# Corner placement of the state-times-q products, and a new order of loads and early weight conversions, in a retention layer followed by two MLPs

## Chip, cores and metric

The kernel runs on one core of a Trainium2 chip. The metric is the device time of one launch in microseconds. The engines are named as in the profile: PE (TensorE matmul), PEld (its weight loads), DVE (VectorE), ACT (ScalarE), POOL (GpSimd) and SP (the queue that issues most transfers).

## The reference, cut to what matters

Retention over 2 batches, 8 heads, 768 positions and head size 64, in blocks along the sequence, with a state carried from block to block; its output, 1536 tokens by 512 channels, goes through two MLPs of 512 to 2048 to 512.

```python
for b in range(nb):
    intra = einsum('bhic,bhjc->bhij', qb, kb) * Dmask
    intra = einsum('bhij,bhjd->bhid', intra, vb)
    inter = einsum('bhid,bhde->bhie', qb * lam_pow, kv_state)
    out[:, :, sl] = intra + inter
    kv_state = lam_block * kv_state + einsum('bhsd,bhse->bhde', kb * rev_pow, vb)
h = x @ w_in;  g = max(h, 0) + alpha * min(h, 0);  x = g @ w_out
h = x @ w_in2; g = max(h, 0) ** 2;                 out = g @ w_out2
```

## The kernel before, in words

**Retention.** The kernel takes chunks of 128 positions, so there are 6 chunks and 2 batches, 12 steps n (`ORDER`, L40), with the batches alternating. A step has four groups of eight float32 products, one per head; the heads go in four pairs `a`, and `t` is the head's place in its pair. `scores(n)` (L393 to L406) multiplies k by q into the tile `s`; `decay(n)` (L408) multiplies that by the decay mask on DVE. `outputs(n)` (L427) holds the other three: `o` from v and the masked scores (L436), `o` from the state and q (L444, from n = 2 on), which adds to the same PSUM tile, and `pk` from r and v (L459, `products`), which is the state's increment; r is k with its rows reversed. `factors(n)` scales q and r on POOL (L418, L421), two steps ahead. In L444 head t takes partitions 64t to 64t+63 of the contraction and writes the same partitions of the output, so it uses two corners of the array: top left and bottom right.

**Leaving PSUM.** `keep_output` writes `o` rounded to fp32r (`xah`, ACT, L469); `keep_rest` writes the remainder (`xal`, L479): on DVE, or, in a step that also converts weights, on POOL from a full copy that ACT made (`whole`, L472). `keep_state` adds `pk` to the decayed old state (DVE, L485) and decays the new state for two steps later (`old`, four ACT instructions, L491).

**Weights.** The weights come as float64 bits, in 64 pieces of 512 KB (`load_piece`, `raw`). A conversion makes a high and a low fp32r part, in program order: L127 and L128 on ACT (`start`), L134 and L135 on DVE (`begin`), L143 on DVE and L145 on ACT, which writes `wh` (`middle`), L154 on DVE, which writes `wl` (`end`). `SEQ` is the order of the pieces. Four conversions lie inside retention, at the steps that `EARLY_UNITS` (L44) marks; `EARLY_LOADS` (L45) marks the steps at which a piece is loaded on SP. The rest is converted one per MLP step and loaded on ACT's queue.

**MLPs.** A step computes `h` (L176, 12 matmuls), its activation (L185 to L195) and, two steps later (`LAG`), adds to four accumulators `acc` (L229, 12 matmuls). PE gets three `h` groups first, then `acc` of the first, and from there on one `h` and one `acc` group by turns.

**What sets the order.** The schedule is written by hand: every engine runs its instructions in the order of the program text, from L495 on for retention. Pools limit how far ahead it goes: two PSUM tiles each for `s`, `o` and `pk`, three tiles for `raw`. `keep_warm` puts dummy matmuls (`warm`) on PE at the start.

Of the kernel before, what the change touches and what calls it, by code (L numbers as in the profile page):

```python
# [7 lines left out]
F32 = mybir.dt.float32  # L8
# [4 lines left out]
ALU = mybir.AluOpType  # L13
PSUM = bass.MemoryType.PSUM
# [14 lines left out]
LA = 3  # L29
# [10 lines left out]
ORDER = [(n // B, n % B) for n in range(NN)]  # L40

REBIAS = 2.0**-112
WARM = 12, 8
EARLY_UNITS = [0, 0, 0, 1, 0, 1, 0, 1, 0, 1, 0, 0]  # L44
EARLY_LOADS = [1, 0, 1, 0, 1, 0, 1, 0, 1, 1, 1, 0]  # L45

STEPS = [(m, t, f, p) for m in range(2) for t, p in PARTS[m] for f in p]
USES = [
# [10 lines left out]
def retention_then_two_mlps(  # L59
# [50 lines left out]
    def load_piece(queue=nc.scalar):  # L110
        if len(loaded) < 4 * NF:
            j = SEQ[len(loaded)]
            loaded.append(j)
            raws[j] = raw = rawp.tile([128, DM, 2], U32, tag="raw", name=f"raw{j}")
            w = (w1, w2)[j // (2 * NF)]
            queue.dma_start(raw.rearrange("p a b -> p (a b)"), w[j % (2 * NF)])

    class Conversion:
        def __init__(self):
# [162 lines left out]
    psk = actx.enter_context(tc.tile_pool(name="psk", bufs=2, space=PSUM))  # L282

# [18 lines left out]
    def load_vk(n):  # L302
        v_t = kp.tile([128, H, D], F32, tag="v", name=f"v{n}")
        nc.sync.dma_start(v_t, vr[n])  # L304
        r_t = None
# [3 lines left out]
        vk_t[n] = v_t, r_t  # L309


    warm = ap1.tile([128, CH], F32, name="warm")
    nc.gpsimd.memset(warm, 0.0)

    def keep_warm(i):
        pw = pso.tile([128, NPAIR, CH], F32, tag="o", name=f"warm_ps{i}")
        for a in range(WARM[i]):
            nc.tensor.matmul(pw[:, a % NPAIR, :], warm, warm, start=True, stop=True)

    def where(name, shape, pattern, base, fill, channel=1):  # L320

# [14 lines left out]
    eye = where("eye", [H, H], [[-1, H]], 0, 1.0)  # L336

    keep_warm(0)
    for n in range(FIRST - 1):
        load_qk(n)  # L340
    load_vk(0)

    lams = lam_sb.to_broadcast([H, CH])
    before, after = power[:, 0:CH], power[:, 1 : CH + 1]
# [25 lines left out]
    fade = ap1.tile([128, H, 1], F32, name="fade")  # L370

    def growth():
        pg = psk.tile([128, 2, NPAIR, D], F32, tag="pk", name="pg")
        pg = pg.rearrange("p a b c -> p (a b c)").rearrange("p (a i) -> p a i", i=CH)
# [6 lines left out]
        pf = pso.tile([128, NPAIR, CH], F32, tag="o", name="pf")[:, 0, 0:H]  # L381
        nc.tensor.matmul(pf, z[:, CH - 1 : ZW - 1], eye, start=True, stop=True)
        nc.vector.tensor_copy(fade[:, :, 0], pf)

# [37 lines left out]
                r_t, r_t, fade.to_broadcast([128, H, D]), ALU.mult  # L422
            )

    old_t, pk_t = {}, {}

    def outputs(n):  # L427
        c, b = ORDER[n]
        q_t = qk_t.pop(n)[0]
        v_t = vk_t[n][0]  # L430
        sc = sc_t.pop(n)[0]
        po = pso.tile([128, NPAIR, CH], F32, tag="o", name=f"o{n}")

# [30 lines left out]
    whole_t = {}  # L464

    def keep_output(n, po):
        ti, cols = n // CPT, slice((n % CPT) * CH, (n % CPT + 1) * CH)
        xh, xl = xt[ti]
        nc.scalar.copy(xh[:, :, cols], po)  # L469
        if EARLY_UNITS[n]:  # L470
            whole_t[n] = whole = ap2.tile([128, NPAIR, CH], F32, tag="whole", name=f"whole{n}")
            nc.scalar.copy(whole, po)  # L472

    def keep_rest(n, po):

        ti, cols = n // CPT, slice((n % CPT) * CH, (n % CPT + 1) * CH)
        xh, xl = xt[ti]
# [156 lines left out]
```

## Time and profile before

| | |
|---|---|
| median of 3 runs | 582.74 us (581.24 to 582.86) |
| the profiled execution's own time | 582.9 us |
| its span | 580.6 us |
| PE busy | 572.1 us (99%) |
| DVE / ACT / POOL busy | 334.7 / 293.6 / 33.3 us |
| retention, to the first `h` matmul | 0 to 54.4 us |
| chain that ended last | PE 95%, DMA 3%, DVE 1% |

The span runs from the first to the last instruction of the profile; the run's own time is 2.3 us longer. Times in rows are microseconds from the start of the span. PE is busy nearly all the time, so what counts is where it was not, and what it waited for there.

### The profile page before, as it was taken

What the parts mean: (1) busy time and instruction counts of PE and PEld (TensorE: products, weight loads), DVE (VectorE), ACT (ScalarE), POOL (GpSimd) and SP (SyncE); (2) the same over time, 40 slices, a digit from 0 to 9 for tenths busy, and PEclk for the clock granted to TensorE, in tenths of its full rate; (3) what the DMA queues carried; (4) which work ended last, traced back from release to release, by engine and by line L of the source; (5) the groups of instructions that cost most, each with busy time, mean ns of one, the idle gap of its engine ahead of it and who ended that gap; (6) DMA issues with size and microseconds to landing.
All of it is one profiled execution on the core that took longest, in us unless ns stands there. A gap on an engine that the chain in (4) does not pass through costs nothing.

```text
span 580.6 us, 7855 instructions
## 1 busy us (share of the span) xinstructions
PE 572.1 (99%) x3058; PEld 475.7 (82%) x3058; DVE 334.7 (58%) x535; ACT 293.6 (51%) x509; POOL 33.3 (6%) x34
## 2 busy tenths in 40 slices
PE   8998999999999999999999999999999999999997
PEld 7887888888888888888888888888888888888885
DVE  3888766666666666866866965665632222222422
ACT  2566765765746765765765654654522222322220
POOL 2785000000000000000000000000000000000000
PEclk9999999999999999999999999999999999999999
DMA  7993343323544223333333123423100000400401
GB/s 255 361 393 120 108 146 109 117 102 109 192 147 168 82 100 109 110 108 110 108 110 109 51 94 110 141 78 109 73 0 1 0 1 0 146 0 1 145 2 72
DMA packets 25732, 62.38 MB, mean 107 GB/s; under 512 B 2904, under 2 KB 3936, under 8 KB 25696
## 3 DMA queue, kind: packets, MB, share of 16 engines
q1 hardware_dynamic: 17488, 32.01, 15.7%
q10 hardware_dynamic: 8208, 29.89, 15.5%
q8 instruction: 24, 0.39, 0.3%
q14 instruction: 12, 0.10, 0.0%
HBM read 52.44 MB, written 9.45 MB: 107 GB/s over the span
## 4 chain that ended last, share of the span: by engine, by line
PE 95%; DMA 3%; DVE 1%; issue 0%; SPq 0%; DVEq 0%
PE h L176 45%; PE acc L231 22%; PE acc L229 22%; PE o L436 2%; PE o L444 2%; PE s L399 1%; DMA q<-in_qt_dram 1%; DMA r<-in_kr_dram 1%; DMA zd<-z 1%; PE pk L459 1%; DMA lam_sb<-in_lam_dram 0%; DVE err L358 0%; DVE ps L245 0%; SPq L304 0%; DVE low L359 0%
## 5 line engine op out<-in xcount | busy, mean ns | idle before, releaser
L195 ACT CAST gh<-g 128x512 fp32r<-128x512 f32 x96 | 59.6, 621 | 90.5 <-DVE g L186 37.5
L186 DVE SCALAR_TENSOR_TENSOR g<-h,g 128x512 f32<-128x512 f32 x48 | 33.2, 691 | 123.4 <-ACT g L185 123.4
L185 ACT ACTIVATE g<-h 128x512 f32<-128x512 f32 x48 | 28.7, 598 | 124.3 <-PE h L176 124.3
L200 DVE TENSOR_TENSOR gl<-g,gh 128x512 fp32r<-128x512 f32 x96 | 66.5, 692 | 30.3 <-ACT gh L195 21.6
L176 PE MATMUL h<-xah,wl 128*128 128x512 f32 x192 | 74.8, 390 | 0.0
L176 PE MATMUL h<-xah,wh 128*128 128x512 f32 x192 | 74.7, 389 | 0.0
L176 PE MATMUL h<-xal,wh 128*128 128x512 f32 x192 | 74.7, 389 | 0.0
L229 PE MATMUL acc<-gh,wl 128*128 128x512 f32 x192 | 74.7, 389 | 0.0
L229 PE MATMUL acc<-gh,wh 128*128 128x512 f32 x192 | 74.7, 389 | 0.0
L229 PE MATMUL acc<-gl,wh 128*128 128x512 f32 x192 | 74.7, 389 | 0.0
L176 PE MATMUL h<-xbh,wl 128*128 128x512 f32 x192 | 74.7, 389 | 0.0
L176 PE MATMUL h<-xbl,wh 128*128 128x512 f32 x192 | 74.7, 389 | 0.0
L176 PE MATMUL h<-xbh,wh 128*128 128x512 f32 x192 | 74.7, 389 | 0.0
L231 PE MATMUL acc<-wl,gh 128*128 128x512 f32 x192 | 74.7, 389 | 0.0
L231 PE MATMUL acc<-wh,gh 128*128 128x512 f32 x192 | 74.7, 389 | 0.0
L231 PE MATMUL acc<-wh,gl 128*128 128x512 f32 x192 | 74.7, 389 | 0.0
L190 DVE SCALAR_TENSOR_TENSOR g<-h,g 128x512 f32<-128x512 f32 x42 | 29.0, 691 | 62.2 <-ACT g L189 62.2
L135 DVE SCALAR_TENSOR_TENSOR bits<-raw,bits 128x512 uint32<-128x512 uint32 x64 | 46.9, 733 | 2.2
L154 DVE TENSOR_TENSOR wl<-bits,wh 128x512 fp32r<-128x512 f32 x64 | 44.6, 697 | 2.7 <-ACT wh L145 2.7
L143 DVE CUSTOM_DVE_ANT_0 bits<-raw,bits 128x1024 uint16<-128x1024 uint16 x64 | 46.0, 718 | 0.0
L127 ACT ACTIVATE bits<-raw 128x512 f32<-128x512 f32 x64 | 43.0, 672 | 0.7 <-DMA raw<-in_w_dram 0.6
L128 ACT ACTIVATE raw<-raw 128x512 int32<-128x512 uint32 x64 | 42.7, 667 | 0.0
(73 smaller groups left out, 786.4 us busy)
## 6 DMA issues: line engine op xcount, KB each, us to landing
raw<-in_w_dram ACTq DMA_DIRECT2D x57, 512.0 KB, 3.3
ps<-sums SPq DMA_DIRECT2D x24, 256.0 KB, 3.1
sums<-p SPq DMA_DIRECT2D x20, 256.0 KB, 2.2
raw<-in_w_dram SPq DMA_DIRECT2D x7, 512.0 KB, 6.3
k<-in_kt_dram SPq DMA_DIRECT2D x12, 256.0 KB, 5.9
q<-in_qt_dram SPq DMA_DIRECT2D x12, 256.0 KB, 5.3
v<-in_vr_dram SPq DMA_DIRECT2D x12, 256.0 KB, 6.0
r<-in_kr_dram SPq DMA_DIRECT2D x10, 256.0 KB, 5.7
```

Of the source, the lines that this page charges most:

```text
L127: nc.scalar.activation(x.bitcast(F32), high.bitcast(F32), AF.Copy, scale=REBIAS)
L128: nc.scalar.activation(low.bitcast(I32), low, AF.Copy, scale=2.0**-29)
L135: nc.vector.scalar_tensor_tensor(x, high, 0x80000000, x, ALU.bitwise_and, ALU.bitwise_or)
L143: nc.vector.tensor_tensor(x.bitcast(I32), x.bitcast(I32), low.bitcast(I32), ALU.add)
L154: nc.vector.tensor_tensor(lo, x, hi.bitcast(F32), ALU.subtract)
L176: nc.tensor.matmul(ph, w[:, cols], x[:, c, :], start=c == 0 and i == 0, stop=c == NC - 1 and i == 2)
L186: nc.vector.scalar_tensor_tensor(g, ph, 0.0, g, ALU.max, ALU.mult)
L190: nc.vector.scalar_tensor_tensor(g, ph, 0.0, g, ALU.max, ALU.subtract)
L195: nc.scalar.copy(gh, g)
L200: nc.vector.tensor_tensor(gl, g, gh.bitcast(F32), ALU.subtract)
L229: nc.tensor.matmul(acc[t][i], w[:, cols], g, **flags)
L231: nc.tensor.matmul(acc[t][i], g[:, cols], w, **flags)
```

## The change

It does five things.

- L444's products: in odd pairs (a = 1, 3) the output goes to the other half of the partitions, so these pairs use the array's other two corners, and their outputs lie in a second PSUM bank. `o`, in two banks now, shares its tile with `pk`; the pool `psk` is gone. L436's products swap halves with them.
- In steps with a state, `pk` is computed ahead of `o` instead of behind it.
- The channel halves of odd pairs are swapped in x by this. To match, the halves are swapped back in the first MLP's `w_in` pieces (even j below 32), which come in three transfers in place of one.
- `keep_rest` is always on DVE, ahead of `keep_state`; `whole` and POOL's part are gone.
- Early conversions move from steps 3, 5, 7, 9 to 4, 7, 10, 11, early loads from 0, 2, 4, 6, 8, 9, 10 to 1, 4, 6, 7, 8, and two pieces are loaded on ACT's queue at 10 and 11. At the head, loads and `scores(3)` stand in another order, and there are 5 dummy matmuls in place of 8.

```diff
-WARM = 12, 8
-EARLY_UNITS = [0, 0, 0, 1, 0, 1, 0, 1, 0, 1, 0, 0]
-EARLY_LOADS = [1, 0, 1, 0, 1, 0, 1, 0, 1, 1, 1, 0]
+WARM = 12, 5
+EARLY_UNITS = [0, 0, 0, 0, 1, 0, 0, 1, 0, 0, 1, 1]
+EARLY_LOADS = [0, 1, 0, 0, 1, 0, 1, 1, 1, 0, 0, 0]
...
+            if j < 2 * NF and j % 2 == 0:
+                to = flat.rearrange("p (i o e) -> p i o e", o=2, i=NPAIR // 2)
+                of = w.rearrange("p (i o e) -> p i o e", o=2, i=NPAIR // 2)
+                queue.dma_start(to[:, :, 0], of[:, :, 0])
+                queue.dma_start(to[0:D, :, 1], of[D : 2 * D, :, 1])
+                queue.dma_start(to[D : 2 * D, :, 1], of[0:D, :, 1])
+            else:
+                queue.dma_start(flat, w)
...
-    for n in range(FIRST - 1):
+    for n in range(2):
         load_qk(n)
-    load_vk(0)
...
     nc.sync.dma_start(zd, z)
-    load_qk(FIRST - 1)
+    load_qk(2)
+    load_v(0)
     nc.sync.dma_start(dec, bass.AP(zd[:, :].tensor, zd[:, :].offset, [[1, 128], [ZW, H], [1, CH]]))
...
-        po = pso.tile([128, NPAIR, CH], F32, tag="o", name=f"o{n}")
+        bank = pso.tile([128, 2, NPAIR, CH], F32, tag="o", name=f"o{n}")
+        pk = bank[:, 1, 2:].rearrange("p a i -> p (a i)").rearrange("p (a d) -> p a d", d=D)
+        if c == 0:
+            po = bank[:, 0].rearrange("p (i o) t -> p o i t", o=2)
+        else:
+            po = bank[:, :, 0:2]
+            if c < NCH - 1:
+                products(n, pk)
+        def half(a, t):
+            return slice((t ^ a & 1) * D, ((t ^ a & 1) + 1) * D)
...
-                        po[d, a, :], state[b, c % 2][d, a, :], q_t[d, a, :], start=False,
-                        stop=True, skip_group_check=True,
+                        po[half(a, t), a % 2, a // 2, :], state[b, c % 2][d, a, :], q_t[d, a, :],
+                        start=False, stop=True, skip_group_check=True,
...
-        nc.scalar.copy(xh[:, :, cols], po)
-        if EARLY_UNITS[n]:
-            whole_t[n] = whole = ap2.tile([128, NPAIR, CH], F32, tag="whole", name=f"whole{n}")
-            nc.scalar.copy(whole, po)
+        nc.scalar.copy(x_view(xt[n // CPT][0], n), po)
...
-        engine, full = (nc.gpsimd, whole_t.pop(n)) if n in whole_t else (nc.vector, po)
-        engine.tensor_tensor(xl[:, :, cols], full, xh.bitcast(F32)[:, :, cols], ALU.subtract)
+        nc.vector.tensor_tensor(x_view(xl, n), po, x_view(xh.bitcast(F32), n), ALU.subtract)
...
-    for n in range(FIRST):
-        scores(n)
-        if n == 1:
-            growth()
-    load_vk(1)
+    load_r(0)
+    load_v(1)
+    load_qk(FIRST - 1)
+    load_r(1)
+    scores(0)
+    scores(1)
+    growth()
+    scores(2)
...
         keep_output(n, po)
+        keep_rest(n, po)
         if pk is not None:
             keep_state(n, pk)
-        if n not in whole_t:
-            keep_rest(n, po)
         if EARLY_UNITS[n]:
             if n >= NN - 2:
                 conv.begin()
-            conv.middle(load=False)
+            conv.middle(load=n >= NN - 2)
             conv.end()
```

PE, the step n = 8 with the scores of 11 behind it, before (`o8`, `pk8`, `s11` are tiles of those steps):

```order
L436 MATMUL o8_730<-sc8_601,v8_606 64x128 x8
L444 MATMUL o8_730<-q8_478,state0_0_194 64x128 x8
L459 MATMUL pk8_747<-v8_606,r8_608 64x64 x8
L399 MATMUL s11_764<-q11_662,k11_663 128x128 x8
L436 MATMUL o9_778<-sc9_661,v9_666 64x128 x8
```

And now:

```order
L477 MATMUL o8_707<-v8_581,r8_583 64x64 x8
L455 MATMUL o8_707<-sc8_576,v8_581 64x128 x8
L463 MATMUL o8_707<-q8_458,state0_0_185 64x128 x8
L408 MATMUL s11_737<-q11_638,k11_639 128x128 x8
L477 MATMUL o9_749<-v9_642,r9_644 64x64 x8
```

The group of r and v went from the third place to the first, and writes the tile `o8`.

ACT, from the output of step 10 to the first activation of the MLP, before (`bits`, `raw` and `wh` belong to conversions, `xah2` is the output rounded):

```order
L145 CAST wh1_812<-bits1_760 128x512
L469 CAST xah2_88<-o10_820 128x4x128
L469 CAST xah2_88<-o11_839 128x4x128
L127 ACTIVATE bits6_858<-raw6_728 128x512
L128 ACTIVATE raw6_728<-raw6_728 128x512
L127 ACTIVATE bits3_875<-raw3_776 128x512
L128 ACTIVATE raw3_776<-raw3_776 128x512
L188 ACTIVATE g0_0_0_893<-h0_0_0_880 128x512
```

And now:

```order
L487 CAST xah2_88<-o10_782 128x2x2x128
L153 CAST wh4_804<-bits4_778 128x512
L124 DMA raw3_806<-in_w1_dram 128x1024
L135 ACTIVATE bits1_810<-raw1_646 128x512
L136 ACTIVATE raw1_646<-raw1_646 128x512
L487 CAST xah2_88<-o11_813 128x2x2x128
L153 CAST wh1_835<-bits1_810 128x512
L124 DMA raw5_837<-in_w1_dram 128x1024
L135 ACTIVATE bits6_841<-raw6_703 128x512
L136 ACTIVATE raw6_703<-raw6_703 128x512
L135 ACTIVATE bits3_857<-raw3_806 128x512
L136 ACTIVATE raw3_806<-raw3_806 128x512
```

Two conversions' `wh`, one pair of L135 and L136 and two transfers now stand between the output of step 10 and the first activation.

DVE, the same place, now:

```order
L492 TENSOR_TENSOR xal2_89<-o10_782,xah2_88 128x2x2x128
L142 TENSOR_SCALAR bits4_778<-bits4_778 128x512
L143 SCALAR_TENSOR_TENSOR bits4_778<-raw4_585,bits4_778 128x512
L151 ISA bits4_778<-raw4_585,bits4_778 128x1024
L162 TENSOR_TENSOR wl4_808<-bits4_778,wh4_804 128x512
L492 TENSOR_TENSOR xal2_89<-o11_813,xah2_88 128x2x2x128
L142 TENSOR_SCALAR bits1_810<-bits1_810 128x512
L143 SCALAR_TENSOR_TENSOR bits1_810<-raw1_646,bits1_810 128x512
L151 ISA bits1_810<-raw1_646,bits1_810 128x1024
L162 TENSOR_TENSOR wl1_839<-bits1_810,wh1_835 128x512
```

The remainder of output 10 has a whole conversion behind it, and so has that of output 11; before, these two remainders followed each other behind the conversion of step 9.

## Rows read from the trace of the kernel before

**Rows 1.** Windows: busy us (instructions) of PE, PEld, DVE, ACT, POOL; granted clock; DMA share; GB/s

```profile
30.00:40.00 10.00, 10.00 (x170) 8.64 (x172) 9.16 (x11) 5.87 (x16) 8.78 (x7) 1.00 1.04 393
40.00:50.00 10.00, 8.66 (x154) 7.29 (x150) 9.24 (x12) 7.46 (x18) 9.28 (x8) 1.00 0.71 260
54.50:62.50 8.00, 8.00 (x36) 6.61 (x37) 6.32 (x11) 7.18 (x14) 0.00 (x0) 1.00 0.36 110
```

**Rows 2.** The chain that ended last, 22 to 63 us: start, length, what

```profile
22.33 1.16 PE s L399 x16
23.50 1.02 PE o L436 x16
24.52 1.02 PE o L444 x16
25.54 0.62 PE pk L459 x16
...
48.69 1.56 issue
50.25 1.09 PE o L436 x16
51.34 1.02 PE o L444 x16
...
54.41 8.38 PE h L176 x36
```

**Rows 3.** Timeline of DVE, 44 to 61 us: start, length, instruction [idle before, releaser]

```profile
44.90 1.50 DVE L143 CUSTOM_DVE_ANT_0 bits<-raw,bits 128x1024 uint16<-128x1024 uint16 x1
47.08 1.00 DVE L154 TENSOR_TENSOR wl<-bits,wh 128x512 fp32r<-128x512 f32 x1 [0.69 <-ACT wh L145]
48.01 1.21 DVE L411 TENSOR_TENSOR sc<-s,dec 128x1024 f32<-128x1024 f32 x1
49.14 0.41 DVE L485 TENSOR_TENSOR state<-pk,old 128x256 f32<-128x256 f32 x1
49.47 0.68 DVE L479 TENSOR_TENSOR xal<-o,xah 128x512 fp32r<-128x512 f32 x1
...
56.11 0.42 DVE L134 TENSOR_SCALAR bits<-bits 128x512 uint32<-128x512 uint32 x1
56.56 0.69 DVE L135 SCALAR_TENSOR_TENSOR bits<-raw,bits 128x512 uint32<-128x512 uint32 x1
...
59.39 0.68 DVE L143 CUSTOM_DVE_ANT_0 bits<-raw,bits 128x1024 uint16<-128x1024 uint16 x1
60.16 0.69 DVE L200 TENSOR_TENSOR gl<-g,gh 128x512 fp32r<-128x512 f32 x1
```

**Rows 4.** Timeline of POOL, 44 to 46 us

```profile
44.81 1.04 POOL L421 TENSOR_TENSOR r<-r,fade 128x512 f32<-128x512 f32 x1 [0.72 <-DMA r<-in_kr_dram]
45.81 1.72 POOL L479 TENSOR_TENSOR xal<-whole,xah 128x512 fp32r<-128x512 f32 x1
```

**Rows 5.** Timeline of ACT, 45 to 60 us

```profile
45.07 1.06 ACT L491 ACTIVATE old<-state,grow 128x64 f32<-128x64 f32 x4 [1.04 <-DVE state L485]
...
46.96 0.58 ACT L469 CAST xah<-o 128x512 fp32r<-128x512 f32 x1
...
53.65 0.62 ACT L145 CAST wh<-bits 128x512 fp32r<-128x512 f32 x1 [3.99 <-DVE bits L143]
...
55.13 0.68 ACT L127 ACTIVATE bits<-raw 128x512 f32<-128x512 f32 x1
...
57.40 0.59 ACT L188 ACTIVATE g<-h 128x512 f32<-128x512 f32 x1
...
59.50 0.62 ACT L195 CAST gh<-g 128x512 fp32r<-128x512 f32 x1 [0.76 <-DVE g L190]
```

**Rows 6.** Timeline of PE: dummy matmuls on the whole array, and the first `acc` matmul

```profile
13.08 2.05 PE L318 MATMUL warm_ps<-warm 128*128 128x128 f32 x16
...
62.63 0.39 PE L229 MATMUL acc<-gh,wl 128*128 128x512 f32 x1
```

More of the change, by code (lines that the diff above doesn't have):

```diff
@@ L114, in load_piece @@
             raws[j] = raw = rawp.tile([128, DM, 2], U32, tag="raw", name=f"raw{j}")
-            w = (w1, w2)[j // (2 * NF)]
-            queue.dma_start(raw.rearrange("p a b -> p (a b)"), w[j % (2 * NF)])
+            w = (w1, w2)[j // (2 * NF)][j % (2 * NF)]
+            flat = raw.rearrange("p a b -> p (a b)")
+            if j < 2 * NF and j % 2 == 0:
[6 more added lines that the diff above has]
+                queue.dma_start(flat, w)
     class Conversion:
@@ L281, in retention_then_two_mlps @@
     pso = actx.enter_context(tc.tile_pool(name="pso", bufs=2, space=PSUM))
-    psk = actx.enter_context(tc.tile_pool(name="psk", bufs=2, space=PSUM))
     lam_sb = ap1.tile([H, 1], F32, name="lam_sb")
@@ L300, in load_qk, with load_v, load_r @@
         qk_t[n] = q_t, k_t
-    def load_vk(n):
+    def load_v(n):
         v_t = kp.tile([128, H, D], F32, tag="v", name=f"v{n}")
         nc.sync.dma_start(v_t, vr[n])
-        r_t = None
+        vk_t[n] = v_t, None
+    def load_r(n):
         if ORDER[n][0] < NCH - 1:
@@ L308, in load_vk @@
             nc.sync.dma_start(r_t, kr[n])
-        vk_t[n] = v_t, r_t
+            vk_t[n] = vk_t[n][0], r_t
     warm = ap1.tile([128, CH], F32, name="warm")
@@ L315, in keep_warm @@
     def keep_warm(i):
-        pw = pso.tile([128, NPAIR, CH], F32, tag="o", name=f"warm_ps{i}")
+        pw = pso.tile([128, 2, NPAIR, CH], F32, tag="o", name=f"warm_ps{i}")
         for a in range(WARM[i]):
-            nc.tensor.matmul(pw[:, a % NPAIR, :], warm, warm, start=True, stop=True)
+            nc.tensor.matmul(pw[:, 0, a % NPAIR, :], warm, warm, start=True, stop=True)
     def where(name, shape, pattern, base, fill, channel=1):
@@ L372, in growth @@
     def growth():
-        pg = psk.tile([128, 2, NPAIR, D], F32, tag="pk", name="pg")
-        pg = pg.rearrange("p a b c -> p (a b c)").rearrange("p (a i) -> p a i", i=CH)
+        pgf = pso.tile([128, 2, NPAIR, CH], F32, tag="o", name="pgf")
+        pg = pgf[:, 0]
         for a in range(NPAIR):
@@ L380, in growth @@
         nc.vector.tensor_copy(grow, pg)
-        pf = pso.tile([128, NPAIR, CH], F32, tag="o", name="pf")[:, 0, 0:H]
+        pf = pgf[:, 1, 0, 0:H]
         nc.tensor.matmul(pf, z[:, CH - 1 : ZW - 1], eye, start=True, stop=True)
@@ L423, in factors @@
             )
-    old_t, pk_t = {}, {}
+    old_t = {}
     def outputs(n):
@@ L436, in outputs @@
                 nc.tensor.matmul(
-                    po[t * D : (t + 1) * D, a, :], v_t[:, 2 * a + t, :], sc[:, t, a, :],
-                    start=a == 0, stop=c == 0, skip_group_check=True,
+                    po[half(a, t), a % 2, a // 2, :], v_t[:, 2 * a + t, :], sc[:, t, a, :],
+                    start=a == 0 or a == 1 and c == NCH - 1, stop=c == 0, skip_group_check=True,
                 )
@@ L444, in outputs, with products @@
                     nc.tensor.matmul(
-                        po[d, a, :], state[b, c % 2][d, a, :], q_t[d, a, :], start=False,
-                        stop=True, skip_group_check=True,
-                    )
-        if c < NCH - 1 and n not in pk_t:
-            products(n)
+                        po[half(a, t), a % 2, a // 2, :], state[b, c % 2][d, a, :], q_t[d, a, :],
+                        start=False, stop=True, skip_group_check=True,
+                    )
+        elif c < NCH - 1:
+            products(n, pk)
         vk_t.pop(n)
-        return po, pk_t.pop(n, None)
-    def products(n):
+        return po, pk if c < NCH - 1 else None
+    def products(n, pk):
         v_t, r_t = vk_t[n]
-        pk_t[n] = pk = psk.tile([128, 2, NPAIR, D], F32, tag="pk", name=f"pk{n}")[:, 0]
         for a in range(NPAIR):
@@ L462, in products, with x_view @@
                 )
-    whole_t = {}
+    def x_view(x, n):
+        cols = slice((n % CPT) * CH, (n % CPT + 1) * CH)
+        return x.rearrange("p (i o) t -> p o i t", o=2)[:, :, :, cols]
     def keep_output(n, po):
-        ti, cols = n // CPT, slice((n % CPT) * CH, (n % CPT + 1) * CH)
-        xh, xl = xt[ti]
-        nc.scalar.copy(xh[:, :, cols], po)
-        if EARLY_UNITS[n]:
-            whole_t[n] = whole = ap2.tile([128, NPAIR, CH], F32, tag="whole", name=f"whole{n}")
-            nc.scalar.copy(whole, po)
+        nc.scalar.copy(x_view(xt[n // CPT][0], n), po)
     def keep_rest(n, po):
-        ti, cols = n // CPT, slice((n % CPT) * CH, (n % CPT + 1) * CH)
-        xh, xl = xt[ti]
-        engine, full = (nc.gpsimd, whole_t.pop(n)) if n in whole_t else (nc.vector, po)
-        engine.tensor_tensor(xl[:, :, cols], full, xh.bitcast(F32)[:, :, cols], ALU.subtract)
+        xh, xl = xt[n // CPT]
+        nc.vector.tensor_tensor(x_view(xl, n), po, x_view(xh.bitcast(F32), n), ALU.subtract)
     def keep_state(n, pk):
@@ L509, in retention_then_two_mlps @@
         if n + 2 < NN:
-            load_vk(n + 2)
+            load_v(n + 2)
+            load_r(n + 2)
         if EARLY_LOADS[n]:
@@ L533, in retention_then_two_mlps @@
             factors(n + 2)
-        if n in whole_t:
-            keep_rest(n, po)
-        if FIRST <= n + LA < NN:
+        if n + LA < NN:
             scores(n + LA)
```

1 line of the change is left out of this document (removed).

## Prediction

> **What bounds the kernel now.** I read the windows first, then the chain, then the timelines of single engines. In the windows from 30 to 50 us DVE and POOL are busy for nearly the whole time, the DMA engines too until 40 us, and PE loses 1.34 us between 40 and 50 us [rows 1]. The chain shows where: PE goes group by group, 1.02 us for eight products of L436 or L444, 0.62 for `pk`, 1.09 for the scores, until 48.69, stands for 1.56 us, takes up step 10 at 50.25 and starts the MLPs at 54.41 [rows 2]. In DVE's timeline the wait has its cause: the conversion of step 7 ends late, the decay of step 10 starts at 48.01, and the remainder of output 8, which frees the PSUM tile that output 10 needs, ends at 50.15 [rows 3]. From 54.41 on no row has PE idle: `h` takes 8.38 us, and the first `acc` matmul starts at 62.63 [rows 2, 6]. ACT is the engine to watch there, busy 7.18 of 8.00 us [rows 1]: it ends the first `gh` at 60.12 [rows 5], and `gl` follows on DVE at 60.85 [rows 3], less than 2 us before PE asks for it. All work behind that point stays as it is, so **the time moves by as much as the first `acc` matmul moves**.
>
> **The change, part by part.**
>
> *Corners.* Ten groups of L444, 1.02 us each [rows 2]. The dummy matmuls on the whole array take 2.05 us for as many records as L436 and L444 have in 1.02 [rows 2, 6], so two products that use different halves already run side by side. With four corners in turn a group would take about half, 0.55 us with its start; the bounds are 0.5 and 1.02, and I take 0.55, because L436 and L444 share two ways without a loss. In steps 2 to 9 this is not on the path (below); in steps 3 and 10 it is.
>
> *`pk` first.* It now waits for r of its step, scaled on POOL, and for DVE to have read the PSUM tile two steps back; behind it stand `o`, L444 and the next scores. The last scaling of r started at 44.81, when its load had just landed [rows 4]. One 512 KB piece fewer is loaded ahead of it (three, not four): 1.33 us at 393 GB/s [rows 1]. The split pieces move the same bytes in more transfers; between no cost and a whole piece's 1.33 us each I take 0.2, near none, since the tensors' own loads, in short runs as well, reach 393 GB/s. So r lands some 0.7 us earlier, and `pk` of step 9 can start at 45.1 at the earliest.
>
> *Head of the program.* The mask's load goes ahead of several others, three dummy matmuls go. Step 3 would end its L444 near 25.5, as before (25.54 [rows 2]): L444 is shorter and the first piece out of the way, but the step's head now waits for r. Bounds: 24.3 (the piece's 1.33 us in full) and 26.
>
> *DVE through steps 4 to 9.* Four subtractions of 0.68 us come to DVE from POOL; two conversions leave it. A conversion costs 0.42 + 0.69 + 0.68 us on DVE when POOL rests, but L143 took 1.50 and L154 1.00 while POOL ran [rows 3, 4]; I take those, and 1.50 for L135, as POOL keeps its scalings. From L444 of step 3 at 25.5: `xah` 0.58, `xal` 0.68, state 0.41, `old` 1.06, L127 0.68 [rows 3, 5], so the conversion of step 4 starts at 28.9. L134 0.42, L135 1.50, `xal` 0.68, state 0.41, L143 1.50, the wait for `wh` 0.69, L154 1.00: 35.1, less overlaps of 0.08 between neighbours: 34.8. Then decay 1.21, `xal`, state: 36.9; `old` and `xah`: 38.6; `xal`, state: 39.7; `old` and L127: 41.4. There the conversion of step 7 starts; with L135 half disturbed (1.1) it ends 5.4 us later, at 46.8. Decay of step 10, `xal` and state of step 8 take 2.1 more, and they free the tile: output 10 starts at 48.9, **1.35 us earlier than 50.25**. Its L444 ends at 48.9 + 1.02 + 0.55 = 50.5; before, at 52.36.
>
> *The tail.* Now two conversions lie behind outputs 10 and 11, and ACT takes them in program order ahead of the MLP's first activation, so each waits for DVE in turn. From L444 of step 10: `xah` 0.58, `xal` 0.68, L134 0.42, L135 0.69, L143 0.68, `wh` 0.62 = 3.67; L127 and L128 of the next conversion 1.14 (half of 57.40 - 55.13); the same 3.67 for output 11; two more pairs 2.27; then from the activation's start to the end of `gh` 2.72 (57.40 to 60.12) [rows 3, 5]: 13.5 us, POOL being done by then. `acc` uses `gl` in its third matmul, so 0.3 more: `acc` can run from 50.5 + 13.8 = **64.3**. PE itself would be there at about 50.9 (the tile for output 11) + 1.6 + 8.38 [rows 2] = 60.9 and stands for some 3.4 us. `acc` moves from 62.63 to 64.3, by 1.7 us.
>
> *At no cost:* the split loads inside the MLPs (DMA share 0.36 there [rows 1]), the missing `whole` copies (ACT has room until step 9), the PSUM pools (as many banks as before). If ACT's room were gone in the MLPs, a step would be late by its extra transfers' issue, but they come after the first `gh`.
>
> **Sum.** Corners, head and DVE bring L444 of step 10 forward by 1.9 us; of the tail, 62.63 - 52.36 = 10.3 us becomes 13.8. Net +1.7: 582.9 (the profiled execution's own time) + 1.7 = **584.6**. The median of the three runs is 582.74, 0.2 lower; a measurement of this kernel can tell about 0.3%, 1.75 us, from no change, so the bounds are 580.99 and 584.49, and the forecast lies a little above the upper one.
>
> **Rivals.**
>
> *Only two corners at a time.* L444 stays at 1.02; then steps 3 and 10 each lose 0.47: 585.5. For it: no row has more than two products side by side. Against it: L436's two halves share all rows of the array and still take no longer than L399's, which share no row (1.02 and 1.09 for 16 [rows 2]). The Trainium skill has a rule that would bring this about (TensorE: Matmul & The Clock Gate, Part 3: Packing small matmuls): a weight load overlaps running matmuls only where its row group is another one. By it the third corner, in the row group of the first, would wait, and the group would stay at 1.02; L436's rows speak against it in this breadth. Chance 0.17.
>
> *Not slower: the conversions run free.* POOL has four products fewer, its idle time may fall where DVE converts, and the DVE chain above shrinks by up to 1.9 us per conversion (0.81 + 0.82 + 0.31). Then r of step 9 sets the end: `pk` at 45.1, 0.62 + 1.02 + 0.55 to the end of step 9, 1.02 + 0.55 for step 10: 48.9, and `acc` at 62.7: no change, 582.9. It decides once L444 of step 10 ends before 48.8. For it: POOL waits 0.72 us for r even now [rows 4]. Against: both conversions that follow a scaling were disturbed. Chance 0.22.
>
> *The clock falls in the wait before `acc`.* The granted clock is 1.00 in every window here [rows 1], but the longest wait in them is 1.56 us [rows 2]. At the lower level (1.2 in place of 2.4 GHz) one group of 12 matmuls, 8.38 / 3 = 2.8 us, takes 2.8 more: 587.4. The Trainium skill (TensorE: Matmul & The Clock Gate, HAM oscillation) warns of idle gaps in the middle of a kernel as the cause of such a fall; no run here shows one. Chance 0.12.
>
> *The head gains more than I see*, 2 us or more with r early, and output 10 runs by 47: 580.9. r's load speaks against it. Chance 0.10.
>
> **How the numbers follow.** The forecast's own case has 0.39; it lies within 0.8 us of 584.6, so 0.21 of it is slower by over 0.3% and 0.18 is not. Only two corners: 0.15 and 0.02. Free conversions: 0.19 within, 0.03 faster. Clock: 0.12 slower. Head: 0.10 faster. Together: faster 0.13, same 0.39, slower 0.48. The range goes from 581.6, under the free conversions by their own spread, to 587.3, which takes in most of the clock's case; it leaves out the head, the rest of the clock's and the ends, some 0.19.
>
> **What would show it.** In the profile after: sixteen records of L463 (L444 now) in about 0.55 us; PE idle in front of output 10, DVE's `xal` or state the releaser; the first activation near 61 us with two `wh` on ACT between output 10 and it; PE idle for 3 to 4 us in front of the first `acc`, released by ACT or DVE, and none after; granted clock 1.00. The prediction is wrong if output 10 starts before 47.5 or after 50.5, if `acc` does not wait, or if PE waits later in the MLPs.

## The result: slower by 1.3%, and the profile after

The changed kernel takes 589.95 us, the median of four runs (588.38 to 591.32), against 582.80 in the same job: ratio 1.0133, 95% interval 1.0117 to 1.0150. The forecast was 584.6, so the direction was right and the size was not. The profiled execution is the fastest of the four, 588.38 us with a span of 586.5, which is 5.9 more than before. No profile shows the 1.4 to 2.9 us that the others lost beyond it.

First the windows of the changed kernel, same columns as in [rows 1].

```profile
30.00:40.00 10.00, 8.81 (x182) 7.47 (x182) 8.19 (x12) 4.45 (x14) 7.28 (x6) 1.00 1.08 328
40.00:50.00 10.00, 8.05 (x163) 6.64 (x161) 8.37 (x11) 4.70 (x14) 7.10 (x6) 1.00 0.90 274
...
60.00:70.00 10.00, 6.80 (x22) 4.83 (x22) 7.28 (x13) 8.33 (x15) 0.00 (x0) 0.83 0.30 105
```

From 30 to 40 us the DMA engines are as busy as before (1.08 and 1.04), but move 328 GB/s where they moved 393, and PE, gapless before, loses 1.2 us. From 60 to 70 us PE is busy for 6.8 us, and the granted clock is below 1.00. The timeline of PE tells what it waits for. In the sense of [rows 2]: L477 is `pk`, L455 and L463 are the two groups of `o` (L436 and L444 before), L184 is `h`, L237 `acc`.

```profile
28.45 0.69 PE L477 MATMUL o<-v,r 128*64 128x64 f32 x16 [1.24 <-POOL r L430]
...
39.30 0.69 PE L477 MATMUL o<-v,r 128*64 128x64 f32 x16 [1.19 <-POOL r L430]
...
47.75 0.69 PE L477 MATMUL o<-v,r 128*64 128x64 f32 x16 [1.52 <-POOL r L430]
48.26 1.04 PE L455 MATMUL o<-sc,v 128*64 128x128 f32 x16
49.24 0.67 PE L463 MATMUL o<-q,state 64*64 64x128 f32 x16
49.83 1.09 PE L455 MATMUL o<-sc,v 128*64 128x128 f32 x16
50.86 0.67 PE L463 MATMUL o<-q,state 64*64 64x128 f32 x16
...
53.33 0.50 PE L184 MATMUL h<-xah,wl 128*128 128x512 f32 x1
...
65.01 0.50 PE L237 MATMUL acc<-gh,wl 128*128 128x512 f32 x1 [3.20 <-ACT gh L203]
...
68.02 0.63 PE L237 MATMUL acc<-gh,wh 128*128 128x512 f32 x1
...
69.73 0.40 PE L184 MATMUL h<-xah,wl 128*128 128x512 f32 x1
...
90.81 0.50 PE L237 MATMUL acc<-gh,wl 128*128 128x512 f32 x1 [1.16 <-ACT p L258]
```

For comparison, the first `h` matmul behind the first `acc` group (62.63, [rows 6]) in the kernel before:

```profile
65.35 0.39 PE L176 MATMUL h<-xah,wl 128*128 128x512 f32 x1
```

The span's 5.9 us stand in these rows. `acc` starts at 65.01 in place of 62.63: 2.38. Its first group lasts until 69.73, 4.72 us where it took 2.72 before (62.63 to 65.35), with matmuls of 0.63 in place of 0.39: 2.00. Ahead of 90.81 PE stands once more for 1.16; with the slower start behind it, the rest of the program takes 1.49 longer. Together 5.87, of which 3.49 lie behind the start of `acc`. The middle one is the clock:

```profile
65.00:69.75 4.75, 4.74 (x13) 3.48 (x14) 4.00 (x7) 3.96 (x7) 0.00 (x0) 0.64 0.29 110
69.75:75.00 5.25, 5.25 (x25) 4.31 (x24) 3.11 (x6) 3.08 (x6) 0.00 (x0) 1.00 0.33 100
```

It fell behind the 3.20 us wait, to a mean of 0.64 over the first `acc` group, and was back at 1.00 for the next `h`. ACT's timeline shows both what `acc` waited for and what comes at 90 us (against [rows 5]; ACTq rows are transfers that ACT issues):

```profile
54.72 0.62 ACT L153 CAST wh<-bits 128x512 fp32r<-128x512 f32 x1 [2.54 <-DVE bits L151]
...
59.48 0.62 ACT L153 CAST wh<-bits 128x512 fp32r<-128x512 f32 x1 [2.54 <-DVE bits L151]
...
62.24 0.59 ACT L196 ACTIVATE g<-h 128x512 f32<-128x512 f32 x1
...
64.34 0.62 ACT L203 CAST gh<-g 128x512 fp32r<-128x512 f32 x1 [0.76 <-DVE g L198]
...
68.69 0.62 ACT L203 CAST gh<-g 128x512 fp32r<-128x512 f32 x1 [0.76 <-DVE g L198]
69.29 0.62 ACT L153 CAST wh<-bits 128x512 fp32r<-128x512 f32 x1
69.29 0.64 ACTq L120 DMA_DIRECT2D raw<-in_w_dram  x1
69.97 0.62 ACTq L121 DMA_DIRECT2D raw<-in_w_dram  x1
70.62 0.62 ACTq L122 DMA_DIRECT2D raw<-in_w_dram  x1
71.29 0.69 ACT L135 ACTIVATE bits<-raw 128x512 f32<-128x512 f32 x1 [1.38 <-issue]
...
74.53 0.62 ACT L203 CAST gh<-g 128x512 fp32r<-128x512 f32 x1 [0.76 <-DVE g L198]
...
80.35 0.62 ACT L203 CAST gh<-g 128x512 fp32r<-128x512 f32 x1 [0.76 <-DVE g L198]
...
89.65 0.62 ACT L203 CAST gh<-g 128x512 fp32r<-128x512 f32 x1 [2.20 <-DVE g L201]
90.17 2.04 ACT L258 COPY p<-acc 128x512 f32<-128x512 f32 x4
```

Both late `wh` wait for DVE, as forecast. In the MLPs a step with an even piece issues three transfers, and ACT stands for 1.38 us before its next instruction: from one `gh` to the next it takes 5.84 and 5.82 us, while PE needs 2 x 2.72 = 5.44 for its two groups. So ACT falls behind by 0.4 a step, and what it does at 90.17, the copies of finished sums, comes late. (The 2.20 us that it waits for DVE at 89.65 belong to the same lag: DVE's L198, one step before, had waited 2.08 us for ACT.) The late tail has its part in this: ACT begins the first activation only at 62.24. The one step here with a single transfer takes ACT 4.35 us (64.34 to 68.69), so without the split it would win back 1.1 us a step.

### The profile page after: what moved, and what is told of

Its sections match the earlier page's. It is cut to its first block, busy times and chain, and to the rows that moved or that the text cites. A ratio compares the mean times of both kernels' runs of the same rounds, so it can differ in the third digit from the quotient of the medians.

```text
span 586.5 us, 7884 instructions
## 1 busy us (share of the span) xinstructions
PE 570.6 (97%) x3052; PEld 472.5 (81%) x3052; DVE 333.2 (57%) x539; ACT 291.2 (50%) x505; POOL 27.3 (5%) x30
## 4 chain that ended last, share of the span: by engine, by line
PE 84%; DMA 6%; ACT 4%; DVE 2%; issue 1%; SPq 1%; ACTq 1%; POOL 0%; DVEq 0%; POOLq 0%
PE h L184 41%; PE acc L239 22%; PE acc L237 20%; DMA raw<-in_w_dram 2%; DMA q<-in_qt_dram 2%; DMA r<-in_kr_dram 1%; DMA v<-in_vr_dram 1%; ACT raw L136 1%; ACT g L197 1%; DVE g L198 1%; ACT gh L203 1%; ACT bits L135 1%; ACT g L196 0%; ACT wh L153 0%; ACTq L121 0%
## 5 line engine op out<-in xcount | busy, mean ns | idle before, releaser
L237 PE MATMUL acc<-gh,wl 128*128 128x512 f32 x192 | 75.5, 393 | 4.4 <-ACT gh L203 3.2
L237 PE MATMUL acc<-gl,wh 128*128 128x512 f32 x192 | 75.6, 394 | 0.0
L237 PE MATMUL acc<-gh,wh 128*128 128x512 f32 x192 | 75.2, 392 | 0.0
L184 PE MATMUL h<-xah,wl 128*128 128x512 f32 x192 | 74.8, 390 | 0.0
L184 PE MATMUL h<-xal,wh 128*128 128x512 f32 x192 | 74.7, 389 | 0.0
L184 PE MATMUL h<-xah,wh 128*128 128x512 f32 x192 | 74.7, 389 | 0.0
L184 PE MATMUL h<-xbl,wh 128*128 128x512 f32 x192 | 74.7, 389 | 0.0
L184 PE MATMUL h<-xbh,wl 128*128 128x512 f32 x192 | 74.7, 389 | 0.0
L184 PE MATMUL h<-xbh,wh 128*128 128x512 f32 x192 | 74.7, 389 | 0.0
L198 DVE SCALAR_TENSOR_TENSOR g<-h,g 128x512 f32<-128x512 f32 x42 | 29.0, 691 | 65.3 <-ACT g L197 65.3
L135 ACT ACTIVATE bits<-raw 128x512 f32<-128x512 f32 x64 | 43.0, 672 | 14.9 <-issue 13.5
L237 PEld LDWEIGHTS acc<-gh,wl 128*128 128x128 f32 x192 | 36.4, 190 | 12.7 <-ACT gh L203 3.6
L143 DVE SCALAR_TENSOR_TENSOR bits<-raw,bits 128x512 uint32<-128x512 uint32 x64 | 45.1, 704 | 2.2
L162 DVE TENSOR_TENSOR wl<-bits,wh 128x512 fp32r<-128x512 f32 x64 | 44.2, 690 | 3.0 <-ACT wh L153 3.0
L151 DVE CUSTOM_DVE_ANT_0 bits<-raw,bits 128x1024 uint16<-128x1024 uint16 x64 | 44.3, 692 | 0.1
```

The lines of the kernel that those rows point to most:

```text
L135: nc.scalar.activation(x.bitcast(F32), high.bitcast(F32), AF.Copy, scale=REBIAS)
L143: nc.vector.scalar_tensor_tensor(x, high, 0x80000000, x, ALU.bitwise_and, ALU.bitwise_or)
L151: nc.vector.tensor_tensor(x.bitcast(I32), x.bitcast(I32), low.bitcast(I32), ALU.add)
L162: nc.vector.tensor_tensor(lo, x, hi.bitcast(F32), ALU.subtract)
L184: nc.tensor.matmul(ph, w[:, cols], x[:, c, :], start=c == 0 and i == 0, stop=c == NC - 1 and i == 2)
L198: nc.vector.scalar_tensor_tensor(g, ph, 0.0, g, ALU.max, ALU.subtract)
```

## The experiments

Ratios are to the kernel before in the same job (its median was 582.06 to 582.27). All have their 95% interval.

### What the split transfers cost

**One transfer per piece** (`w` is then laid out with the halves already swapped):

```diff
-            if j < 2 * NF and j % 2 == 0:
+            if False:
```

> The changed kernel, but the two halves of odd pairs are swapped where the weights are laid out ahead of the launch, so every piece comes in one transfer. Theory (three losses: two conversions ahead of the first activation 2.4 us, the clock's fall in the wait behind it 2.0 us, ACT's extra issues in the MLPs 1.5 us): the 1.16 us wait of PE near 90 us is gone, ACT's MLP steps that load an even piece lose about 1.9 us each, r of step 9 lands earlier by up to 1 us, the wait of some 3 us before the first acc and the slow records behind it stay: 587.5 to 588.5 us. Rival (the wait at 90 us is the two sums' copies on ACT and has nothing to do with the loads): it stays, 589.5 to 590 us.

587.36 us, 1.0080 (1.0059 to 1.0102): some 2.6 us less than the changed kernel (3.1 by the ratios), and no wait near 90 us. In retention the rate is back, and r with it; the `pk` of step 9 starts at 44.78, not 47.75. First the window, then PE, with the wait that now comes next, and the DVE and POOL rows behind that one (the profiled execution took 589.08, 1.7 over the median and the slowest of six):

```profile
30.00:40.00 10.00, 9.32 (x188) 8.02 (x188) 8.31 (x11) 4.61 (x13) 8.42 (x8) 1.00 1.04 389
```

```profile
44.78 0.69 PE L477 MATMUL o<-v,r 128*64 128x64 f32 x16
...
50.19 1.98 PE L455 MATMUL o<-sc,v 128*64 128x128 f32 x16 [3.25 <-issue]
```

```profile
46.22 1.80 DVE L162 TENSOR_TENSOR wl<-bits,wh 128x512 fp32r<-128x512 f32 x1 [1.11 <-ACT wh L153]
47.95 1.21 DVE L420 TENSOR_TENSOR sc<-s,dec 128x1024 f32<-128x1024 f32 x1
49.08 0.67 DVE L492 TENSOR_TENSOR xal<-o,xah 128x512 fp32r<-128x512 f32 x1
49.68 0.41 DVE L498 TENSOR_TENSOR state<-o,old 128x256 f32<-128x256 f32 x1
```

```profile
44.45 3.02 POOL L427 TENSOR_TENSOR q<-q,grow 128x512 f32<-128x512 f32 x2
```

With r on time, DVE sets output 10, as the prediction had it: the end of step 7's conversion takes 1.80 us beside POOL's scalings, and state 8 frees the tile just before 50.19. This profile has one more loss: behind the wait the group at 50.19 takes 1.98 us, where that of step 9 took 1.07, since the granted clock fell.

```profile
50.19:52.10 1.91, 1.91 (x17) 1.58 (x17) 1.91 (x3) 0.00 (x0) 0.00 (x0) 0.50 0.00 0
```

So the first `h` starts at 54.93, later than in the changed kernel (53.33), although r comes earlier.

**The split alone, in the kernel before** (same bytes, same places, three transfers):

```diff
+                queue.dma_start(to[:, :, 0], of[:, :, 0])
+                queue.dma_start(to[0:D, :, 1], of[0:D, :, 1])
+                queue.dma_start(to[D : 2 * D, :, 1], of[D : 2 * D, :, 1])
```

> The kernel before, with each even piece of the first MLP's weights in three transfers in place of one, the same bytes to the same places. Theory (the split costs by itself): in retention the DMA engines move less (some 330 in place of 390 GB/s while busy), r of the late steps lands later and PE waits for it; in the MLPs ACT spends 1.9 us more in each step that loads an even piece, is over the 5.44 us of a PE step, and PE waits where the sums are copied: 1.5 to 5 us slower, 584 to 588 us. Rival (transfers of the same bytes cost the same, ACT has the room): within 0.5 us, 582 to 583 us.

585.77, 1.0056 (1.0044 to 1.0068): 3.5 us for the split by itself. Its rate from 30 to 40 us and its first `h` (56.23; 54.34 before) show the one half, a wait of 0.9 on the copies of the sums the other; the third fence is the view of waits (total, times, longest).

```profile
30.00:40.00 10.00, 7.79 (x128) 6.47 (x128) 9.28 (x11) 5.54 (x14) 6.91 (x5) 1.00 1.04 318
```

```profile
56.23 0.50 PE L184 MATMUL h<-xah,wl 128*128 128x512 f32 x1
```

```profile
PE acc L237 <- ACT p L258: 0.9, 1, 0.9
```

**Its two ways apart.** The swapped layout again, three transfers only on SP's queue (retention), or only on ACT's (MLPs):

```diff
-            if j < 2 * NF and j % 2 == 0:
+            if j < 2 * NF and j % 2 == 0 and queue is not nc.scalar:
```

> The changed kernel with the halves swapped ahead of the launch and the even pieces in three transfers only where SP loads them, in retention (three of the five); in the MLPs one transfer per piece. Theory (two ways of costing, each about half): against the kernel with one transfer (587.4) it loses what r's delay costs in retention, 1 to 1.5 us; there is no wait near 90 us: 588 to 589 us. Rival (all of it is ACT's issues): 587 to 587.6. Rival (all of it is the transfers' rate): 589.5 to 590 us.

> The complement: one transfer in retention, three for each even piece that ACT loads. Theory: retention as with one transfer, the wait near 90 us of 1.2 to 2 us comes back, since ACT's steps with an even piece take 5.83 us against 5.44 of PE: 588.3 to 589.5 us. Rival (the wait at 90 us is only what the late tail leaves, the rate alone costs): 587 to 587.6 us.

588.43, 1.0111 (1.0094 to 1.0129), and 589.18, 1.0120 (1.0100 to 1.0140): 1.1 and 1.8 us over one transfer everywhere. (Four of the five pieces that SP loads are even, not three.) Both intervals still touch that of the kernel with one transfer, so the shares are rough; that each way is there is in the rows. The first has 340 GB/s from 30 to 40 us, `pk` of step 9 at 48.47 and no wait near 90; the second has 390 GB/s, `pk` at 43.86 and this:

```profile
PE acc L237 <- ACT gh L203: 3.0, 1, 3.0
PE acc L237 <- ACT p L258: 1.1, 1, 1.1
```

In retention the second is the same as the kernel with one transfer, and it shows how far executions differ there: output 10 starts at 48.16 and not at 50.19, and its clock stays at 1.00.

```profile
48.16 1.09 PE L455 MATMUL o<-sc,v 128*64 128x128 f32 x16 [2.14 <-issue]
```

### What the late conversions cost

**The new lists in the kernel before** (remainders 10 and 11 on DVE, loads at 10 and 11):

```diff
-EARLY_UNITS = [0, 0, 0, 1, 0, 1, 0, 1, 0, 1, 0, 0]
+EARLY_UNITS = [0, 0, 0, 0, 1, 0, 0, 1, 0, 0, 1, 1]
...
```

> The kernel before, with the changed kernel's lists of early conversions (steps 4, 7, 10, 11) and loads, the remainders of outputs 10 and 11 on DVE; everything else as before. Theory (the tail alone costs): the first activation waits for both late conversions, acc starts 13 to 14 us after L444 of step 10, near 65 to 66 in place of 62.6, PE stands some 3 us ahead of it, the granted clock falls behind that wait and costs up to 2.0 more: 586 to 588 us. Rival (the tail is hidden behind the h groups; loads and corners cost the time): 582 to 583.5 us.

585.12, 1.0047 (1.0034 to 1.0061), less than the 586 to 588 expected. The wait is there with its full size, and the slow group behind it (4.23 us), but two conversions fewer in steps 3 to 9 leave PE without a wait above 0.3 us from 16.3 us to the first `h`, which starts 2.5 us earlier than before:

```profile
51.86 0.50 PE L176 MATMUL h<-xah,wl 128*128 128x512 f32 x1
...
63.36 0.80 PE L229 MATMUL acc<-gh,wl 128*128 128x512 f32 x1 [3.05 <-ACT gh L195]
```

So the lists take with one hand and give with the other; here they cost 2.9 us.

**The clock kept up.** 13 dummy matmuls behind the third `h` group, in the changed kernel and in the one just shown:

```diff
             ph = first(m, t, f)
+            if s == LAG:
+                keep_clock(weights[0][1], x_of[0, 0][0])
```

> The changed kernel with 13 dummy matmuls of 512 columns behind the third h group, in the wait before the first acc; their outputs are not used. Theory: the granted clock stays at 1.00 there, the first acc group takes 2.72 in place of 4.72 us, acc starts at 65.0 as before, the wait at 90 us stays: 2.0 us faster than the changed kernel, 587.5 to 588.3 us. Rival (the slow group is an operand that comes late, not the clock): no change, 589.5 to 590 us.

> The kernel before with the late conversions (as in the first run of that kind: acc at 63.36 after a wait of 3.05 us, first acc group 4.40 us, 585.1 us), and 13 dummy matmuls of 512 columns in that wait. Theory (the slow group is the clock, and nothing else binds right behind it): granted clock 1.00, the group takes 2.72, 583.2 to 583.8 us. Rival (ACT or DVE sets the pace behind the first acc, so the clock's loss is hidden, as in the changed kernel with dummies): within 0.5 of 585.1.

590.64, 1.0148 (1.0132 to 1.0165), and 584.59, 1.0047 (1.0033 to 1.0060). The clock did stay at 1.00 and the first group took 3.1 us in both, and neither kernel got faster by a measurable amount. In the changed kernel the reason is plain: ACT sets the pace until the sums' copies, so what PE saves it waits for there, 2.05 us in place of 1.16: from the start of `acc` to the end of that wait it is 25.8 us in both kernels, whatever the clock.

```profile
62.41 3.11 PE L192 MATMUL dummy<-xah,wl 128*128 128x512 f32 x13
65.79 0.50 PE L242 MATMUL acc<-gh,wl 128*128 128x512 f32 x1 [0.28 <-ACT gh L208]
...
91.61 0.50 PE L242 MATMUL acc<-gh,wl 128*128 128x512 f32 x1 [2.05 <-ACT p L263]
```

In the other, no such wait follows. Its profiled execution is 0.9 us faster, its median 0.5, its ratio the same; what the fall costs there stays open between 0 and 1 us.

**The conversions where they were**, in the changed kernel and in the one with one transfer:

```diff
-EARLY_UNITS = [0, 0, 0, 0, 1, 0, 0, 1, 0, 0, 1, 1]
+EARLY_UNITS = [0, 0, 0, 1, 0, 1, 0, 1, 0, 1, 0, 0]
...
```

> The changed kernel with the early conversions and loads at the steps of the kernel before (3, 5, 7, 9 and 0, 2, 4, 6, 8, 9, 10). Theory: nothing stands between output 11 and the first activation but two pairs of L135 and L136, so acc starts at the end of the third h group, PE has no wait there, the clock stays at 1.00: 2.4 and 2.0 us come back, 585 to 586 us, if retention ends where it does now (53.3); with five loads in retention's first half as before, r lands later, up to 1.3 us more. Rival (the new corners or the order of pk cost the time): 589 to 590 us.

> The changed kernel with one transfer per piece and the early conversions and loads at the steps of the kernel before. Theory: no wait ahead of acc and the clock at 1.00; but all four conversions and all remainders lie on DVE through steps 3 to 9, POOL takes none, so DVE sets the end of retention: the first h near 55 to 57, 583 to 585.5 us. Rival (with the loads in one piece DVE has room): the first h near 52, 580 to 581 us. Rival (the placing of the conversions does not matter): as the changed kernel with one transfer, 587 to 588 us.

588.99, 1.0122 (1.0103 to 1.0140), and 586.23, 1.0076 (1.0062 to 1.0089). No wait ahead of the first `acc` in either, as expected, but both expectations were too low: with the split pieces earlier, the first `h` comes at 61.96 (in its slowest execution, 591.66); with one transfer, at 57.96, behind a wait of 2.14 us for DVE's tile and a fall of the clock. It seems that without POOL's share of the remainders four conversions do not fit into steps 3 to 9, so that the late places answer a real shortage; no run gives POOL its share back with the rest as it is, so this is argued and not shown.

### What the corners are worth

**Two corners** (with one transfer, as nothing is swapped):

```diff
-            return slice((t ^ a & 1) * D, ((t ^ a & 1) + 1) * D)
+            return slice(t * D, (t + 1) * D)
```

> The changed kernel with the natural halves for all pairs: L463 uses the corners (top left, bottom right) alone, two PSUM banks stay, pieces come in one transfer as nothing has to be swapped back. Theory: against the kernel with one transfer, L463 takes 1.02 in place of 0.60 us; steps 3 to 9 wait for r anyway, steps 10 and 11 lose 0.42 each: 0.5 to 0.9 us slower than that kernel. Rival (the corners share nothing that matters): within 0.3 us of it. Rival (a column change between pairs costs weight loads): faster than it.

586.85, 1.0085 (1.0070 to 1.0099): no different from four corners with one transfer. L463 takes 1.09 us here and 0.67 there, and none of it comes through: with four corners PE waits for DVE ahead of output 10, and behind it the tail decides. The expected 0.5 to 0.9 us was wrong.

```profile
22.68 1.09 PE L463 MATMUL o<-q,state 64*64 64x128 f32 x16
```

### A tail in another order

**Late conversions first** (one transfer; `wh` and its DVE part ahead of outputs 10 and 11, both started at step 9):

```diff
+        if late:
+            conv.middle()
         keep_output(n, po)
+        if late:
+            conv.end()
         keep_rest(n, po)
...
```

> The changed kernel with one transfer per piece, and the conversions of steps 10 and 11 ahead of the copies and remainders of outputs 10 and 11 on ACT and DVE, both started at step 9. Theory (the tail is the order in which ACT and DVE take turns, not the work in it): the chain to the first gh is 3 us shorter at least, acc follows the third h group with less than 0.5 us of wait, the clock stays at 1.00 there: 580 to 583 us. Rival (the work of two conversions behind step 9 is too long in any order): acc still waits over 1.5 us, 585 to 587 us.

584.41, 1.0036 (1.0022 to 1.0050): 3 us better than in the old order, and above the 580 to 583 expected, as `acc` still waits 1.53 us, since DVE is only free at 51.65.

**The same order in the kernel before, and with the corners.** Both start a conversion behind the first activation; the second has the corners, one transfer, `pk` behind `o` and the remainders of steps 4 and 7 on POOL.

```diff
-                conv.start(conv.k + 1)
+                if s > 0:
+                    conv.start(conv.k + 1)
                 conv.begin()
...
                 conv.middle()
+                if s == 0:
+                    conv.start(conv.k + 1)
...
```

> The kernel before with the late conversions (4, 7, 10, 11), none of the rest of the change; the conversions of steps 10 and 11 go ahead of the copies and remainders of outputs 10 and 11, both are started at step 9, and in the first MLP step the start of the next conversion goes behind the activation. Theory (fewer conversions on DVE in steps 3 to 9 free PE, the order of the tail gives it back): the first h at 52 in place of 54.4, acc follows the third h group with under 0.5 us of wait, near 60.4 in place of 62.6: 580 to 581 us. Rival (two late conversions are too long in any order): acc near 62 to 63 with a wait of 1.5 us or more, 582.5 to 584.5 us.

> The changed kernel (four corners, its order at the head) with one transfer per piece, pk behind o again, the remainders of steps 4 and 7 on POOL again, and the tail in the order of the kernel before it in this list. Theory (with r off the path and the tail in order, the corners' 0.4 us a step comes through until DVE binds): the first h at 50 to 51.5, acc near 59 to 60.3, 578.5 to 580.5 us. Rival (DVE binds steps 8 to 10, so shorter PE groups only make PE wait longer): the first h at 52 to 53.5 with a wait ahead of output 10, 580.5 to 582.5 us.

581.66, 0.9990 (0.9979 to 1.0002), and 581.07, 0.9986 (0.9975 to 0.9996), both some 0.6 us above the expected range. `acc` starts at 61.14 and 59.52; a second wait, 0.68 and 0.79 us ahead of the next `acc` group, takes part of it back. Both of these second waits stand behind two pairs of ACT's conversion starts (L127 and L128, or L135 and L136).

**Every start one place earlier or behind the activation**, with four corners and, as the only difference, with two:

```diff
-        if n + 1 < NN and EARLY_UNITS[n + 1] or n == NN - 1:
+        if n + 1 < NN and EARLY_UNITS[n + 1]:
             conv.start(conv.k)
-        if n == NN - 3:
+        if n >= NN - 3:
             conv.start(conv.k + 1)
...
```

> The kernel with corners, pk behind o, one transfer and the tail reordered (581.07 us: acc at 59.52 after a wait of 0.97, and 0.79 more ahead of the second acc), and now each start of a conversion goes one place earlier, or behind the activation in every MLP step. Theory (those two waits are ACT's pairs of L135 and L136): both waits together fall to 0.5 us or less, 579.3 to 580.3 us. Rival (DVE's conversions and remainders bind there): 580.8 to 581.3 us.

> The same kernel as the one before it in this list with the natural halves: L444's products in two corners. Theory (the corners save 0.4 us in each of ten steps where PE binds; DVE takes part of it back): 1 to 3 us slower than it. Rival (DVE binds through steps 4 to 10, the corners only make PE wait): within 0.4 us of it.

579.40, 0.9950 (0.9937 to 0.9963), and 581.47, 0.9991 (0.9983 to 1.0000). The first is faster than both kernels of this case: the second wait is gone, the one ahead of the first `acc` is still 0.86 us, more than the 0.5 expected. The corners are worth 2.1 us in it. The first `h` and the first `acc`, four corners and then two:

```profile
50.29 0.50 PE L184 MATMUL h<-xah,wl 128*128 128x512 f32 x1
...
59.61 0.50 PE L237 MATMUL acc<-gh,wl 128*128 128x512 f32 x1 [0.86 <-ACT gh L203]
```

```profile
52.63 0.50 PE L184 MATMUL h<-xah,wl 128*128 128x512 f32 x1
...
61.04 0.50 PE L237 MATMUL acc<-gh,wl 128*128 128x512 f32 x1
```

## Why the prediction was right in its direction and wrong in its size

**What failed** is the premise that the time moves by as much as the first `acc` matmul moves, since all work behind it stays as it is. `acc` moved by 2.38 us, not far from the 1.7 forecast; the span grew by 5.87. Behind it the slow clock took 2.00 us, and ACT, late from the tail and slowed by the split transfers' issues, held PE once more. The cost of the split, put at 0.2 us a piece in retention and at nothing in the MLPs, is about half of the miss (2.6 of 5.4 us). Part by part:

**Corners: right.** 0.55 us was taken for the group, and it measures 0.59 from start to start (49.24 to 49.83). The rival of two corners at a time is out. The rule of the Trainium skill that would have brought it about (TensorE: Matmul & The Clock Gate, Part 3: Packing small matmuls; a weight load overlaps only where the row group differs) does not hold in that breadth for these rows: half the products share the row half of another and the group still takes 0.59.

**The tail: right.** From the end of L463 of step 10 (51.5) to `acc` (65.01) are 13.5 us; 13.8 was forecast. The wait is 3.20, forecast 3.4, and it starts from the two late `wh` as described. The kernel before with the new lists alone shows the same wait, 3.05.

**`pk` first, and r's load: mis-sized, the first failed step.** The prediction let the split pieces cost 0.2 us, near none, because other loads reached 393 GB/s, and had `pk` of step 9 at 45.1. It started at 47.75, and PE waited for r in six steps. With one transfer it starts at 44.78; three split pieces are loaded ahead of that r, so by these two profiles one costs about 1 us (an estimate). The upper bound that stood beside the 0.2, a whole piece's 1.33 us, was nearer: 65 GB/s less over 10 us is 0.65 MB, at 393 GB/s 1.7 us for the pieces of that window. For the same reason the second group of step 10 ended at 51.5, 0.9 us earlier than the 52.36 of before, and not 1.9.

**Split loads inside the MLPs: the second failed step.** They were put under "at no cost" on the DMA share of 0.36. The DMA had room; ACT, which issues them, had not. The text even named the condition (ACT's room gone, a step late by its extra issues) and dropped it because they come after the first `gh`. But a lag of 0.4 us a step adds up until the sums' copies.

Both are one term, the split: 2.6 us in the changed kernel, 3.5 in the kernel before; how it divides between the two ways is not resolved. With it the forecast would have been 587.2, and 2.8 us of the measured 589.95 remain. The kernel with one transfer shows this rest by itself. In its profile `acc` starts 4.08 us later than before (66.71) and its first group takes 4.58 us, 1.86 more; the two make up the 6.0 us of its span, so there nothing hides the clock's fall. How much of the 2.8 us is the clock stays open, as no run holds it with one transfer in this order.

**The clock: a rival that came true.** Its chance was 0.12 and its price 2.8 us; the group lost 2.00, as the clock came back within it. The Trainium skill's warning about idle gaps (same page, HAM oscillation) agrees with the rows at 65 us, though the length of a gap alone does not tell which waits of these runs were followed by a fall (last section). But it is not 2 us of the result: with the clock held, ACT was waited for instead. The prediction's range, said to take in most of this case, ended at 587.3, just below the 587.4 that the case itself came to.

**DVE through steps 4 to 9: near, where r does not hide it.** In the changed kernel r came later than DVE and hid it. With one transfer in retention, output 10 waits for DVE until 50.19, 49.77 (late conversions first) or 48.16 (split on ACT's queue alone); 48.9 was forecast. In the last of these, L162 of step 7 took 0.69 us beside POOL's scalings and not 1.80; the forecast, with one price for each instruction, came out between the executions, and that is in part luck. The rival of free conversions, which needed L444 of step 10 to end before 48.8, is out: even from 48.16 it ends at 49.9.

**The head:** L463 of step 3 ends at 26.04, forecast 25.5, just above its upper bound of 26.

## What to carry to other kernels

A transfer cut in three is paid twice, once in the rate of the DMA engines where they are saturated, and once on the engine that issues it; ask of both queues whether they have room, and for how many steps in a row. Work moved out of a crowded stretch lands in front of something: before moving it, follow the engines' program order to the first result that the bottleneck needs, and put it where two engines need not take turns. A faster group shows up only when nothing else binds: the corners were worth nothing measurable with the old tail, and 2.1 us with the mended one, `pk` behind `o` and POOL's remainders back.

## What the runs showed of the hardware

- From 30 to 40 us the DMA engines' share is 1.02 to 1.08 in all kernels. In the five with pieces split there (runs of 256 words, 1 KB) they moved 318 to 348 GB/s, in all others (runs of 4 KB) 367 to 393. Whether the short runs or the number of transfers does it is not shown.
- The clock does not go by the length of one wait alone. Behind waits of 3.01 to 3.28 us ahead of the first `acc` it fell in all six profiles that had one. Ahead of output 10, a wait of 3.25 us was followed by a fall to 0.50 in the kernel with one transfer, and left the clock at 1.00 in the kernel with late conversions first. A wait of 2.14 us there was followed by a fall to 0.51 with one transfer and the conversions where they were (this row), and by none with the split on ACT's queue alone.

```profile
53.07 1.98 PE L455 MATMUL o<-sc,v 128*64 128x128 f32 x16 [2.14 <-issue]
```

In the kernel with late conversions first, whose rows follow, the wait of 3.25 us left the clock at 1.00, and one of 1.53 us ahead of `acc` was followed by a group of 4.44 us at a mean of 0.75. What decides between these cases is not shown.

```profile
49.50:52.00 2.50, 1.86 (x36) 1.51 (x38) 2.50 (x5) 0.00 (x0) 0.00 (x0) 1.00 0.00 0
61.90:68.20 6.30, 4.77 (x14) 3.49 (x14) 5.32 (x9) 4.75 (x9) 0.00 (x0) 0.75 0.24 83
```

- One subtraction on DVE (L162, 128x512) took 1.80 us in one execution and 0.69 in another, both times beside one of POOL's scalings of q. That scaling took 1.3 us in the first case and 1.7 in the second.
- Four 64 by 64 corners run with little loss: 16 records in 0.59 us, in two corners 1.02.
